# A planner that knows the port shared by two engines: new assumptions and a new table of due times in a two-layer attention and feed-forward kernel

## The chip, the cores and the metric

The kernel runs on one core of a Trainium2 chip. A core has five engines that run side by side and meet through semaphores: TensorE (PE) multiplies matrices, VectorE (DVE) and ScalarE (ACT) work elementwise and empty PSUM, GpSimd (POOL) does masks and small things, SyncE (SP) issues transfers. The metric is device time in microseconds (us), as the median of several runs; lower is better.

## What is computed

Four stages follow each other on a sequence of 2048 tokens of width 640, in bf16: an attention layer A, a feed-forward layer B, and both again with the same weights. Each adds to its input.

```python
x = x + _A_ref(_layernorm(x), wq, wk, wv, wo, beta)
x = x + _B_ref(_layernorm(x), w1, w2)        # relu(x @ w1) @ w2, inner width 1728
x = x + _A_ref(_layernorm(x), wq, wk, wv, wo, beta)
x = x + _B_ref(_layernorm(x), w1, w2)
```

Attention has 32 heads of width 20 and cuts the sequence into 4 segments of 512 tokens. Inside a segment it is causal softmax attention. A running memory `M`, `z` of earlier segments is read beside it:

```python
for s in range(N):
    p = _softmax(qs @ ks.T * scale + mask)
    a_dot = p @ vs
    a_mem = (phi(qs) @ M) / (phi(qs) @ z + 1e-06)    # phi(t) = t + 1 if t > 0 else exp(t)
    outs.append(g * a_mem + (1.0 - g) * a_dot)       # g = sigmoid(beta), by head
    M = M + phi(ks).T @ vs
    z = z + phi(ks).sum()
```

## The kernel before

The unit of work is a segment of a layer, so there are eight of attention and eight of feed-forward. For a segment, the steps and their lines are:

- Layer norm: statistics on DVE (L858, L859, L860), the inverse root on POOL (L865, L867), the normalised tokens `xn_tok` on DVE (L871). They are turned into `xnT` by a crossbar transpose that SP issues (L847), or in the first segments on PE (L835, with an eviction at L842 on DVE or L843 on ACT).
- Projections on PE: keys and queries (L941; evicted at L928 on DVE or L929 on ACT), values (L988; evicted at L976 or L977). A projection fills five tiles; spare rows of these carry the heads of three further tiles, which a DMA through memory moves to partitions of their own (the relay, L1023 and L1036; in the first segment PE does it, L1086).
- Scores on PE in bursts of four or eight small matmuls (L1280), 160 rounds in all. Each round fills four PSUM banks, X and Y, which two exponentials on ACT (L1291, L1294; 128x1024) empty into `PT`. POOL then cuts the causal triangle (L1270). Four heads' worth is multiplied with the values in a burst of sixteen matmuls (apply, L1362), evicted (L1384 or L1390 on DVE), turned by a crossbar transpose (L1461), normalised on DVE (L1396, L1404, L1409) and added to the memory's part (L1414).
- Memory: keys turned by the crossbar (L1117, L1125), `phi` on ACT and DVE (L1133, L1134, L1136), the product on PE (L1143) and its sum and mask on DVE (L1160, L1163). The read is `phi` of the queries (L1196, L1198, L1200), a product (L1230) and DVE steps (L1215, L1218, L1219).
- Output projection: the result `o_sb` turned into `oT` (L1516, crossbar; L1483 on PE in the first segment), PE (L1526), addition to `x_sb` on DVE (L1468).
- Feed-forward: first product (L1580, and L1592 for the rest of 64 columns), relu on DVE (L1561) or ACT (L1562), second product (L1610), addition on DVE (L1468). The second layer's result is stored by SP (L1570).

Three PSUM banks (MISC) serve all other PE work in turn; X and Y together hold one round of scores. Much of PE's work can thus only start once an eviction has freed a bank.

The order on every engine is fixed before the program exists. A planner (`Sched`) takes all steps as streams of `Op`s, each with one or more possible engines and an assumed duration. It keeps a model time per engine, and again and again places the `Op` that can start first; among equals, the one with the earliest due time. Evictions may go to DVE or ACT, whichever ends first in the model. The due times come from `TABLE`, a compressed list with one number for each `Op`, made before. On the chip no model time matters: each engine takes its instructions in the planned order and waits on semaphores where needed. What the planner assumes therefore acts on the kernel through the order and the choice of engine alone.

The assumptions that matter here: a PE step can start `SEM_NS + PE_MARGIN` after the results it reads (60 + 80 ns); a crossbar transpose occupies SP for `XB_NS + XB_TILE` per tile and lands `XB_LAT` after its turn on the DMA; between `LOAD_FROM` and `LOAD_TO` (15 to 125 us of model time) every transfer of SP takes `LOAD_LAT` longer; the relays move 85 bytes per ns. Where PE would have nothing to do, `_filled` puts multiplications of the identity (L769).

The step in which an `Op` gets its model start is in `_best`:

```python
for k, (e, hold, tail, make) in enumerate(op.alts):
    r = ready + SEM_NS + (PE_MARGIN if e == "pe" else 0.0)
    start = rank = max(self.free[e], r)
```

Of the kernel before, what the change touches and what calls it, by code (L numbers as in the profile page):

```python
# [10 lines left out]
ACT = mybir.ActivationFunctionType  # L11
ALU = mybir.AluOpType

T = 2048
# [120 lines left out]
class Op:  # L135
# [4 lines left out]
    def __init__(self, alts, waits, acq=(), users=1, mode="full", dma=None, early=0.0, hold=()):  # L140
        self.alts = alts
        self.waits = [t for t in waits if t is not None]
        self.acq = acq
        self.hold = hold
        self.users = users
        self.mode = mode
        self.dma = dma
        self.due = -1.0
        self.early = early
        self.patience = PATIENCE  # L150

# [7 lines left out]
PE_MARGIN = 80.0  # L159

XB_NS, XB_TILE, XB_LAT = 200.0, 27.0, 1700.0
# [7 lines left out]
LOAD_FROM, LOAD_TO, LOAD_LAT = 15000.0, 125000.0, 4000.0  # L169
# [18 lines left out]
class Sched:  # L188
    def __init__(self, prog, dues=None):
        self.P = prog  # L190
        self.dues = dues
        self.free = {e: 0.0 for e in ENGS}
        self.t = {}
        self.events = {}
        self.fresh = []
        self.active = []
        self.waiting = {}
        self.cur = None
        self.count = 0
        self.ids = set()  # L200
        self.dma_free = 0.0
        self.mode = "full"
        self.log = []
        self.now = -1.0
        self.fill = None
# [71 lines left out]
    def _best(self, op, resv=None):  # L277
# [10 lines left out]
        for k, (e, hold, tail, make) in enumerate(op.alts):  # L288
            r = ready + SEM_NS + (PE_MARGIN if e == "pe" else 0.0)
            start = rank = max(self.free[e], r)  # L290
# [36 lines left out]
    def run(self):  # L327
        while True:
# [45 lines left out]
            if e == "pe":  # L374
                self.mode = op.mode
            if op.dma is not None:
# [29 lines left out]
c-m!JTaX>qb={}?_U(K7zUR*SCC!W^MglzmNyZopA!IP-86XA>31FvUr$~i-  # L406
n4(+`0jE;=%tstk{z?3i4=PTPj{xOVQnno1<%*wFAWA|J4A@vivOpt&n3raD)?VjyPmicuw{Lf!bN1P1pZ!>SpZgJaiPYsTi6xO==}uffD}5P~
*R&%OcuM7CxW-bInhfBsCOy21WKKRRnLL8~7WyC4E70Rkv?gdfu2<piR?r<spBF(jlf!6lqV3nZA8l7l1J5m4(Svxp7T;}XJq0SMT!yDirsaK|
$DKV5qhBmLakriGMfmK+-CoXTboYRsjcrN=&-
?Jb5<F*k8j&q{KM!6iGANg0#4g@<WenHt_{K6SH(>lH@IJwqD?oQQ#`G}DFLgJ5cjJ8rJ@<fCUABUHl{{?0??=!!APaf}*0fbVj`4NO@wz^U_a  # L410
@B-=r2(^+tIR9oV=;K@N{XA$2cg=VE!1Kw&jF=3ZwT>+76@d!mL-Jt%hGGN5R!7XRgS{&uo?3z}fF(O?QCyb+TXX$EvTEYvdM4?Rt#68{bE8|6
6hp@Alx`Zn+8V_WnM(L~h5}+aZUKp~pku{VqKJId=0Xr2ix+-
Y=g4#lvz4d_RcqmoeiV7=2VeCEq{$NpLv>&e~XqNqdKUZ8afpP8Ri9v}TZU1)o$@6Iq8wHNvj+W0P(hb63%)jyW56YNKZYK0A=)F|27A(wW1xh
t?EQPGu5%*nr$mqE{1?2GL^-pDRdX0&QKq@8HR_tBIB$;eHqT4L}ZU&>V;4NAWoT-ffTD=(h#hXTL{r-
GezQkkmHx+=*)kYaRy=BcM0{T7&qVlfR|bk6?x_^n4!Uy5PA3inE{{qkl?GO{nJ$NGYZ5*iM@EOrl4G>uh-5C2wgYQ+T(e6=?e~B-
q9C5au3%R$L;h`T(qK6q+`UUVV96cYyCLxId};<bU<3yr-
u93BJ$k{aD#yd0A&*i!<P>haITVZX@iDlOqcec!~KGagU<nDZfU1>)6t!okYC1H>xq)WA1j$w~j5<VwAOHfvO9m9kn_R^ds7<ze~b+-
_z60M{IEAO3$@Yiz|3`@>TwJNx53AE9ap?4mM_UK@L$dd(3skp)Kzf72h~~^ZBYJ36^<G_@;G{RBdD$_=rmLM)b9QbS3=u!hHG2dRRd|&bS=n+
^>-9g#Ior@##Mq-
k#Qo`?fJ}y(E?Qb)eYS3fJU{^>5ylsPx_yys75vNJ={rZ<2|ZX(LdK3w>DwPfOY;_Gv@^&cX(w(tbz9SkFny`%_xw{N}yi(Uek1*j@|L^w(EmF  # L420
;%Y6Bz-|`?7CLyYrQ__>s+I(1`0VpgZ?Iy;jn(=y#vX6eyTwW%-%Qag`YQ<Wu>(8jXm-+=PQmk*-
Uwq*GcOgmn3WL>uTEE7Qddj(2QJKwM{b3@698}AJW2&JvCbPI|xrS2Jh3rx58MLOCTxsv{vXv6n3X<;|Vpef}M}V&-pXGk%+<-
dRpa5j)1ERTBondZDy7{Rw#iQ{e`XZu>3c!7qrE7)C13Lc+U59vhW8+Nj3L+l^~t`H!AJANw>Ml;^RVRtA%{xLaR6YPA=zW$wzGXmZ?H6^+2tL
_`kjIKbtk)ufbC_%`^@>!Gc}j(^0y$5Bb$N_#t<Z9d*N9TOP;NVyW4h3%1cH_NiU0FD<yK0|{-+YP)xu(Z~EnpS0h@ep#el4EEo^o-
}Arxkryn@<>SCw{G@DuJC-Wh&<jGd0RAlw*L8Z6nw|JHi9mj6?nRFq1UdYleXejb%lRbT8*E@>qaH;S}XZAuY2CR#U-1}C9E2i-
j{vdhDXeMdcE6d@!Yzwx~SN7hii(jUvIu9`>mEVtE`E(@^#qEnl|}1#Y!Xk$GV(>MOYkJ)<LnoGA=&QE@!ET$7@TNuUcsRy1s<IXVth^1J!l(U
e%ar-S1fiUck#-
VXfv#y@o8acMNP20ePves`sp_@9P${pVqg4>Cc0oxbQ&=o);MbI+*1Q5Ka$P^Iy=j|AZwkWAtUfFiniwA^)TwN1vX2pljMA=Lx*<anSx1cwEES
lzK1<4!UR?m!InhaPe_-1K_0wu1@HJCd6Z&yX)n9`VD<ZY&GZAu-
z0gmh0r7^@QGxxu4RrdNtNK2KpvH>$eO&dILNy<823+`2|SfEHK*J;A>cZqyM9ymR~R`ts$<yr>3XB)O+NI`Wu}Cs(cZCYYaRutNFBb$f=H1zp  # L430
Fn0ZaaZ732@yBwVY>&`w$}=t0PZ10ZM1IN(+5oGiquBnEvPFX9_!H+PkJEiBsxh(7OHt`NpbxkDcLpj52!_sL|nlhW<9{EO`2XUJKrAXT~tkh2
T45qS8A0?u75EK^7LH&f)HT9l{z9%1^b%emBa$s?jvRyAND7Ad9=@`?>^5yMb_RMJwQIRlljf2Rf$jHLSY}4HyT-I_RFH?mI?m^LjU9*I&hR7d
ZSy^jHD^r}S-Tr~`!*9Bo7Y3v4-y-R^^eL;iAt>qxn}6|^pE!d!6~JfEjFoX3jK>VJTLTj4ppH{G&`vIrd+gm%4)-
=6?kdrN#?Zz{aRvD1d{tHAuD;Mua533(WrVA8eRvcc?Q8X3hLGm|E;_<e|_mc3kuY$*jI%P_tZGMg^?EUD!=bMX+obPN7C!_IcNzt6c{pl$hh4
-{G$H!Y{#E3k(BXdlP>K5~h^yx^L+cCnj%(9DokjL7kYM!=PueOMW{<vyh!T6{E4idep;9&N=$ZytN?mzOk0%2ilojrrau8RacwsRxuB%a#JM<
lZVO@se|vZSr&*SgBgVE8dI7;xV4d|7!5&GmdtMP+8$KZB(m>WgB#p!iU$%b3R+6h;=@~R6%oDSJdO)Dq>-
t^Ndqc)?*}Khq#mr!~w0Ql4G?zGSmv(-zuV#_3jk$>UeY{P->8Ozot$JgKw6h3!KIUK8RUWXcKAVSzNW?!7)$IrT-UhOF(F8m~DV^*;!yqKcYs
C&1TAUmbFV%6BQbhkIE6&|G}yUik#{>cV%f;|6P41=qVm#blw>vn$7EV&gW_g@s(e(kD>h_izH-2Eh435Vtb$0Jm#(`vc#x_0_vq*am18m-
0X;~l1&IY4fs3XfzhB3aagfQ?$L!<o&?WF<N^6@xf{OvPWiN4CG)V}hvf!2gl{HaU#+3HMXEltn{$wXMT8o6_}B0@Z|Q#WI1L_tgcViE(TZ9{W
s!b2;hf)<*Y!<U#1wY(hlo6f@cv1?j5QIn|7-  # L440
Al3^q6g>ze?_3SayvH2ENFA}#r2{9cDycdFm{Zpiu)W|_m_a1cGJtc(3MXdZ>c52*2Jp0>^X$SA!k<z-
fM3;KL7Za{mQa{0Px@bOST?126x`qt@HGFHYq@?g})+m@tiwrmxot;D01U}<&I&k(J;@+I^g$D7yI_o9z!SPQ*c`0SC4d*<ss+wk;2)WoWX<vZ
)<qYq%VHnIq-JKakU7V}!cY+L2Qv#PW5ntL+ZADwsY=*6W({y{V5lBQLEh~KBR8nmJ&Uk1fTHKCmt509YdS0L9}%5GTpL@lo3TCAzbY-
N&ity9l@EvO4xyRiPd!RI_=c8@lR@2jCcV>|I<y#e%k<iqNQw?tjJ7P~p69;sIuAJdSRT4i<}I@L!8g?R4vvJyL~F?&@oLK*#HW??nPoec83U+
#%c0qYFP5sm5p@;oJFjmiAu60k%A`BqmBI;(;u@+GY^YtN{iNyx&Rlvoe_tS0#Ph|9y6)ugfvFK`@q;287o5oq&kY8Am2ZE9M+h4qhPj>`~(pL
*xn$}RC1q65*nXpg(X-
Me6ZbRyKC%nlDzPXCB+M*FK_tkv=S>h26VX2R?w3i)a(H@SqB$^?A2Ibxdoc{Md{ka56}RfIjX>r;IH827?F#@j#%Ci5qvm^HvQ`fX<fx6h#b5
$BpB!gyLNXS)(T-qCNOkFVJ_Aju}HoMv&~;kZ7f_Z3=nkCyZq$Y4P3p*F2C;*Ak=JVwh|V+3o_>-8x6UGO_6Y2AkI2jwpKn-Tda^h<Syk}w}_U
hoL?at3I`YLiXszv;mc_?y5S!>pTLO7Gdl4mIT`;Cc>rw2L}uh~Kn0LtjHzqu`~1wsmbX78=(66INzZIp#jc_;r}FGavK`eC_OD0`0b+eR|$L_
<0VV@~r+2_hLVNT_3(7f*nt>=dEHHMu(M^gP8X(>B}a#?^EEji*?@%&WF&~By%k}J<qyPk6Jk`dl&wOduZ{z2X9no^i42w1grTx-kL@Y<IPxz3  # L450
l-Y?lia&4M0eYYxHXBW)__mXf+wv~t9&f8SaX}y8GT!L+Ckmx(&kS=-
*007R;Zf$cxE#na)*f5Dp=_t_bUb+JMEYP?z@r*$|}sM?4yR6T~*<iA42~cB10R$^C1$Nk6zT<=(&gJXJcB0=YI;?b{8m(!YW(X-
yvxB9&&HIkI5b6y-#ay;+^-
$kIM(|)xlv8Emf}Pl(XLq^kT8y_^zwaC(dAX!=Ur0ZV+6Xga=rqf85P5)4LJ!p2dnTa~)z_v%j7^FW*8hv+wI!tG-
UY?S8Bt`&!&z)qh*qT>XuU3P4_C@@OY5)tPgAl?6;uu4}*LTtKpUHXfC#;~O>O{)Z~hNx;C-rYh*OE-ETOaZ&M!OVnMc=z5;&QY+PAqk!{z0i8
zjMOO(pC=0cnC7mkj*R6ubj5g*Zx~TqC2`hI2`#t6^XkMXM(`rE6Nm0=~qaIOBGJ09hhYJioT~s}0i)!DDi%K<ZFUeNmu3E}5W&&Dmmw4OY^qE
joj&bMfF!83UTwW7R3;Z_AJZUi4o6%Zkb)%e3*ooX%v0ls9JFG(Fxrmq91!kBPdbu;&W^{ZB*k%@Y3u^JH1~1%a&N~ikw{c%zFpq1vwu-
DbkvYWq1F)j!o#Ch<`G&LH=YTxnrr^i6%gb(5?t}gR0b-_MuvV1f?WA1t?y_1w_6Bxi9NfQ-ym$@syo8K&8#sGKP2LuZ6U67s@tMM`qjGHB{9s
hnS0i{rt1dQqI_P)~nov&Wjou_~>I0o5j5D|4JC8B9yOeLnm^&r%j<aeUu##)>yy|PDu}_|HReJ6*thoc5-
5q6&kfX5YN%T445?b6Sqv<vBR}1s-  # L460
IhR9vTgC2%c>Xm9X|>tEOQbf=yln?^#hqf6nsaJC*pTZ8`mR9o7a;X9YWghpb%qgj5Y}&z$o%G#TCQ8+`E(U`hNh-Dass_<%rsWBit9MWPKW0e
(7O_`csp9QqQ!jpB)HrP9tJVfDyU9k?kVtV5y7|`!mf;?#jx`Q9VPDR5xq=d<Q!J9s1vL{P4ZN-%?v)GhpeO5Hu4kkd~#X0FuJse5PPf-
^umd9AM-EjrSQ`gP_{Kq;yQ&{9nr)HD5RWa6}?t;p5C^Pwb^NQ#90%bZjUnJOaKqBfWK*;L@w$iEN}_WqoBHlr$Z(w;7F`>kn?+a4>Iy+@YcrZ
EcmYx4VdJc;LdAdg*YK$l)9jY@H__({ef1`B%yX~RE9!T=Tfw1(&33<hj_V8k5r?s849XXZ@a-CR@m00h7S<I)p+jMlG8-
fDRsHYQ`SscL`3KG4XqGW**^|EO0N>PrUAG3lh=$`yw1FBmb7Z@mr~;gh!irSDy!LLpx9(fO1^94uSOKo;Cia$A?8d8*Xd6<GR~3)WZIyW_*zA
s@zi63Dq9lfYB4D#lw6B6JYx0lnxTJ-
e%w%Ag%XIlhJ?|mOG)^QKP8PibGLeN>fE4Ia=hFru1Vm(9;zVqP|ay`R4e2>epHjI$bvuakeepGaEJUh_%027+TuM%lQZ9p9JLmDSXAnTtlsaZ
Rcu?~A0~rX%`*MFjsK}0Eig!poMenLRmwh>oIiKV&qjS)CE$U2(1jM`QlIyhZB)XJn%oSxw8JWzVFf*Af0dARbQoV-
# [22 lines left out]
def dve_ns(n, mode):  # L491
    return 66.0 + n / (0.96 * mode)
# [1212 lines left out]
```

## Time and profile before

| | us |
|---|---|
| median of 3 runs | 570.12 (569.62 to 570.35) |
| the profiled execution | 570.93 |
| its span, first to last instruction | 569.2 |

| engine | line | work | count, mean ns |
|---|---|---|---|
| PE | L1610 | second product of the feed-forward | 896, 299 |
| PE | L1580 | first product | 520, 380 |
| ACT | L1294, L1291 | exponentials of the scores | 320, 1025 to 1032 |
| POOL | L1270 | causal masks | 256, 687 |
| DVE | L1468 | additions to x | 128, 479 |
| DVE | L871 | normalised tokens | 64, 529 |
| DVE | L1561 | relu | 50, 666 |
| DVE | L928 | evicted keys and queries | 48, 685 |
| DVE | L1409 | normalised attention | 24, 877 |

A span is what the program's own instructions cover. The time of a run has some 1.7 us more around it. Matmuls overlap, so that their mean durations add up to more than the time they take; the distance between the starts of neighbours tells the pace. The clock granted to TensorE was 1.00 throughout. The crossbar transposes into `xnT`, `oT` and `otok` landed 2.6 to 5.8 us after the start of their issue (median 2.7 to 3.1, by kind).

### The profile page before, as it was taken

The numbers are of one execution on the slowest core, as the hardware profiler recorded it, in microseconds if no ns is written. First come the engines' busy times: TensorE is split into PE (matmuls) and PEld (weight loads), VectorE is DVE, ScalarE is ACT, GpSimd is POOL, SyncE is SP. The second block draws the span as 40 slices with busy tenths as digits, with TensorE's granted clock in tenths as the row PEclk, the third lists the DMA queues.
The fourth block names the chain that finished last, engine by engine and source line by source line (L and its number), as shares of the span: only waits on it lengthen the run. The fifth ranks groups of instructions, "written<-read, shape, count | busy, mean of one in ns | idle before, by whom it ended". The sixth has DMA issues, their size and how long they took to land.

```text
span 569.2 us, 12508 instructions
## 1 busy us (share of the span) xinstructions
PE 558.4 (98%) x5113; PEld 296.0 (52%) x5113; DVE 425.8 (75%) x1020; ACT 424.5 (75%) x519; POOL 215.4 (38%) x343
## 2 busy tenths in 40 slices
PE   8999999999999999999999999999999999999998
PEld 4454445445554445645446554564444654656655
DVE  6689999999999869876689964898767872725202
ACT  4899899998889978778888887977898677332140
POOL 4374447544444434443334423524233422302000
PEclk9999999999999999999999999999999999999999
DMA  6436859766343446454146831386313820432201
GB/s 219 119 89 144 158 123 156 224 150 109 66 91 70 62 71 88 83 97 80 29 77 112 128 43 20 56 122 105 59 21 62 136 69 1 77 81 43 69 0 47
DMA packets 126609, 50.62 MB, mean 89 GB/s; under 512 B 112120, under 2 KB 124600, under 8 KB 126552
## 3 DMA queue, kind: packets, MB, share of 16 engines
q1 hardware_dynamic: 124568, 42.19, 40.7%
q0 software_dynamic: 1552, 7.29, 4.6%
q8 instruction: 40, 0.66, 0.5%
q10 hardware_dynamic: 432, 0.34, 0.2%
q14 instruction: 17, 0.14, 0.1%
HBM read 15.16 MB, written 7.37 MB: 40 GB/s over the span
## 4 chain that ended last, share of the span: by engine, by line
PE 79%; DVE 12%; ACT 4%; DMA 3%; POOL 1%; issue 1%
PE ps L1610 18%; PE ps L1580 17%; PE ps L941 12%; PE ps L1280 7%; PE ps L1526 7%; PE ps L988 7%; PE ps L1362 6%; ACT PT L1294 2%; DMA oT<-o_sb 2%; DVE xn_tok L871 1%; DVE stats L858 1%; DVE x_sb L1468 1%; DVE stats L859 1%; PE ps L1143 1%; PE ps L1230 1%; DVE ktok L1136 1%
## 5 line engine op out<-in xcount | busy, mean ns | idle before, releaser
L1294 ACT ACTIVATE PT<-ps 128x1024 bf16<-128x1024 f32 x256 | 248.3, 1025 | 46.8 <-PE ps L1280 45.9
L1270 POOL TENSOR_SCALAR_AFFINE_SELECT PT<-PT 128x512 bf16<-128x512 bf16 x256 | 171.5, 687 | 262.7 <-ACT PT L1294 218.4
L1610 PE MATMUL ps<-wb,hT 128*128 128x320 bf16 x896 | 136.2, 299 | 1.0 <-DVE x_sb L1468 1.0
L1580 PE MATMUL ps<-xnT,wb 128*128 128x512 bf16 x520 | 126.8, 380 | 0.2 <-DVE hT L1561 0.2
L1468 DVE TENSOR_TENSOR x_sb<-x_sb,ps 128x320 bf16<-128x320 bf16 x128 | 60.7, 479 | 69.9 <-PE ps L1610 47.3
L1610 PEld LDWEIGHTS ps<-wb,hT 128*128 128x128 bf16 x896 | 83.2, 98 | 39.3 <-issue 7.6
L1580 PEld LDWEIGHTS ps<-xnT,wb 128*128 128x128 bf16 x520 | 48.0, 98 | 57.8 <-issue 7.0
L1291 ACT ACTIVATE PT<-ps 128x1024 bf16<-128x1024 f32 x64 | 62.5, 1032 | 14.4 <-PE ps L1280 14.1
L1562 ACT ACTIVATE hT<-ps 128x512 bf16<-128x512 f32 (+1 forms) x62 | 36.1, 583 | 43.6 <-PE ps L1580 42.8
L941 PE MATMUL ps<-xnT,wq_p 128*128 128x512 bf16 x200 | 57.3, 380 | 0.3 <-DVE o_sb L1219 0.3
L988 PE MATMUL ps<-wv_r,xnT 128*128 128x320 bf16 x320 | 57.2, 300 | 0.0
L941 PE MATMUL ps<-xnT,wk_p 128*128 128x512 bf16 x200 | 56.0, 380 | 0.0
L1526 PE MATMUL ps<-wo_r,oT 128*128 128x320 bf16 x280 | 51.8, 299 | 1.2 <-DMA oT<-o_sb 1.1
L1362 PE MATMUL ps<-PT,va 128*32 128x128 bf16 (+3 forms) x896 | 40.8, 302 | 0.0
L988 PEld LDWEIGHTS ps<-wv_r,xnT 128*128 128x128 bf16 x320 | 29.5, 98 | 18.8 <-issue 2.8
L928 DVE CAST kq<-ps 128x512 bf16<-128x512 f32 x45 | 30.8, 685 | 11.1 <-PE ps L941 10.7
L1561 DVE TENSOR_SCALAR hT<-ps 128x512 bf16<-128x512 f32 (+1 forms) x50 | 33.2, 666 | 7.1 <-PE ps L1580 6.9
L871 DVE TENSOR_SCALAR xn_tok<-x_sb,mv,rstd 128x640 bf16<-128x640 bf16 x64 | 33.3, 529 | 4.1 <-POOL rstd L867 2.7
L1280 PE MATMUL ps<-kq 20*128 20x512 bf16 (+3 forms) x560 | 35.3, 301 | 0.2
L1526 PEld LDWEIGHTS ps<-wo_r,oT 128*128 128x128 bf16 x280 | 26.4, 98 | 16.1 <-issue 2.1
L858 DVE BATCH_NORM_STATS2 stats<-x_sb 128x6 f32<-128x320 bf16 x64 | 29.5, 465 | 1.8 <-DMA x_sb<-in_A_x_dram 1.5
L1362 PEld LDWEIGHTS ps<-PT,va 128*32 128x32 bf16 x896 | 18.9, 96 | 22.7 <-issue 10.2
(113 smaller groups left out, 626.6 us busy)
## 6 DMA issues: line engine op xcount, KB each, us to landing
kq_scr<-kq SPq DMA_DIRECT2D x28, 120.0 KB
kqL<-kq_scr SPq DMA_DIRECT2D x28, 120.0 KB
out_dram<-x_sb SPq DMA_DIRECT2D x16, 160.0 KB, 1.8
wb<-in_B_w_dram POOLq DMA_DIRECT2D x5, 432.0 KB, 4.3
x_sb<-in_A_x_dram POOLq DMA_DIRECT2D x3, 640.0 KB, 5.2
wb<-in_B_w_dram POOLq DMA_DIRECT2D x2, 640.0 KB, 5.4
kq_away<-hT SPq DMA_DIRECT2D x5, 256.0 KB, 3.2
kq<-kq_away SPq DMA_DIRECT2D x5, 256.0 KB, 3.4
```

Source lines behind the costliest of these rows:

```text
L871: tn, bx = yield dve(D, 4, lambda e, a, t=t: e.tensor_scalar(a, x_sb[:, t, :], mv[:, t, 0:1], rstd[:, t:t + 1], ALU.subtract, ALU.mult), [ ...
L941: fn = lambda e, bank, k=k, w_p=w_p, c=c: e.matmul(bank, w_p[:, k, c * 128:(c + 1) * 128], xnT[:, k_, :, k, :], start=(k == 0), stop=(k == ...
L988: fn = lambda e, bank, k=k, i=i, hf=hf: e.matmul(bank[:, 0:320], xnT[:, k_, i, k, :], wv_r[:, k, hf * 320:(hf + 1) * 320], start=(k == 0), ...
L1270: tm = yield pool(590.0, lambda e: e.affine_select(out=reg, in_=reg, pattern=[[0, 4], [1, 128]], compare_op=ALU.is_ge, fill=0.0, base=0, c ...
L1280: fns.append((lambda e, x=x, j=j, hh=hh, N=N, o=o: e.matmul(ps[:, hh, o:o + N], kq(b, gg[x], 0)[32 * hh:32 * hh + DH, 128 * j:128 * j + 12 ...
L1291: fn = lambda e: e.activation(PT[:, :, 2 * k:2 * k + 2, 1024:1280], bs.ap.rearrange("p h (x t) -> p x h t", x=2), ACT.Exp, scale=SCALE)
L1294: fn = lambda e: e.activation(PT[:, items[0], 2 * k:2 * k + 2, c0:c0 + 512], bs.ap, ACT.Exp, scale=SCALE)
L1362: return [(lambda e, hh=hh, j=j: e.matmul(bank[32 * hh:32 * hh + 32, 128 * j:L], v_flat[b][:, (j * H + 8 * hh + g) * E1:(j * H + 8 * hh + ...
L1468: ta = yield dve(320, 1, lambda e: e.tensor_tensor(xa, xa, bk.ap[:, 0:320], ALU.add), [tk], early=HOT)
L1526: fn = lambda e, bank, k=k, hf=hf, o=ot.ap: e.matmul(bank[:, 0:320], o[:, k, :], wo_r[:, k, hf * 320:(hf + 1) * 320], start=(k == 0), stop ...
L1580: fn = lambda e, bank, k=k, dc=dc: e.matmul(bank, w1_r[:, k, dc * 128:(dc + 1) * 128], xnT[:, k_, :, k, :], start=(k == 0), stop=(k == FC ...
L1610: fn = lambda e, bank, dc=dc, q=q, h=h, hf=hf: e.matmul(bank[:, 0:320], h, w2_r[:, q, hf * 320:(hf + 1) * 320], start=(dc == 0), stop=(dc ...
```

## The change

Five assumptions of the planner change, and the table of due times is replaced by another:

- `PE_MARGIN` 80 to 200 ns; `XB_LAT` 1700 to 2300 ns; `LOAD_LAT` 4000 to 2500 ns; the rate of the relays 85 to 80 bytes per ns.
- A port that DVE and POOL share is in the plan. A DVE `Op` is marked `port` where its assumed mode is 2 or 4 (and so are the copies of `permute`). A marked DVE `Op` starts in the model no earlier than the end of POOL's last compute `Op`, and a POOL compute `Op` no earlier than the end of the last marked one on DVE.

No instruction of the computation is added or taken away. Line numbers after the table shift by 12.

```diff
-PE_MARGIN = 80.0
-
-XB_NS, XB_TILE, XB_LAT = 200.0, 27.0, 1700.0
+PE_MARGIN = 200.0
+
+XB_NS, XB_TILE, XB_LAT = 200.0, 27.0, 2300.0
...
-LOAD_FROM, LOAD_TO, LOAD_LAT = 15000.0, 125000.0, 4000.0
+LOAD_FROM, LOAD_TO, LOAD_LAT = 15000.0, 125000.0, 2500.0
...
+        self.port = {"dve": 0.0, "pool": 0.0}
...
             r = ready + SEM_NS + (PE_MARGIN if e == "pe" else 0.0)
+            if e == "dve" and op.port:
+                r = max(r, self.port["pool"])
+            if e == "pool" and op.dma is None and hold:
+                r = max(r, self.port["dve"])
...
                 self.mode = op.mode
+            if e == "dve" and op.port or e == "pool" and op.dma is None and hold:
+                self.port[e] = end
...
 TABLE = """
...
 def dve(n, mode, fn, waits=(), acq=(), extra=0.0, users=1, early=0.0):
-    return Op([("dve", dve_ns(n, mode) + extra, 95.0, one(fn))], waits, acq, users, early=early)
+    return Op([("dve", dve_ns(n, mode) + extra, 95.0, one(fn))], waits, acq, users, early=early, port=mode > 1)
...
-                                           lambda e, o=o, i=i: e.activation(o, i, ACT.Copy)))], w)
+                                           lambda e, o=o, i=i: e.activation(o, i, ACT.Copy)))], w, port=True)
...
-                        tk = yield dma("sp", scw_sem[z][r], 122880, f, ev + sc.old, rate=85.0)
+                        tk = yield dma("sp", scw_sem[z][r], 122880, f, ev + sc.old, rate=80.0)
```

## The prediction

> **What bounds the kernel.** I read the page first, for the share of each engine, then the stretches of the span, then the starts of the TensorE's instructions.
>
> ```profile
> PE 558.4 (98%) x5113; PEld 296.0 (52%) x5113; DVE 425.8 (75%) x1020; ACT 424.5 (75%) x519; POOL 215.4 (38%) x343
> ...
> PE   8999999999999999999999999999999999999998
> ...
> DVE  6689999999999869876689964898767872725202
> ...
> PEclk9999999999999999999999999999999999999999
> ```
>
> PE is busy almost everywhere, with the full clock granted (1.00 in every stretch). But a busy PE can hide waits, since matmuls overlap: a 128x320 one lasts 299 ns and the next starts 136 ns after it. So I took the usual distance between starts for each pair of forms (512 columns 216 ns, 320 columns 136 ns, 128 columns 56 ns, 84 columns 40 ns; 95 ns more ahead of a burst of scores or applies) and added them along the program: **550.8 us**. The first matmul starts at 1.24 us, the last one 3.1 us before the end. The span of 569.2 leaves 14.0 us in which PE started later than it could. Of these, 12.0 us are 42 waits of over 25 ns; the other 2.0 are some 10 ns at many of the 691 matmuls that carry a wait. By stage:
>
> | us of the span | 0-16 | 16-50 | 50-120 | 120-190 | 190-360 | 360-460 | 460-569 |
> |---|---|---|---|---|---|---|---|
> | PE waits, us | 3.41 | 1.13 | 2.10 | 2.15 | 0 | 3.16 | 0 |
>
> The program's span plus 1.7 us around it is the profiled execution's 570.93 us, 0.8 over the median of 570.12. Nothing but these 14.0 us can be won, since the change computes the same thing.
>
> Which engine makes PE wait? The stretches (busy us of PE, PEld, DVE, ACT, POOL) say where each has no room:
>
> ```profile
> 50.00:120.00 70.00, 68.91 (x715) 33.46 (x707) 66.27 (x158) 65.48 (x78) 37.54 (x60) 1.00 0.78 166
> 120.00:190.00 70.00, 68.82 (x708) 36.69 (x701) 68.00 (x162) 61.48 (x71) 30.92 (x46) 1.00 0.49 91
> 190.00:360.00 170.00, 170.00 (x1629) 87.94 (x1630) 132.50 (x300) 139.74 (x166) 68.96 (x103) 1.00 0.43 71
> ```
>
> From 120 to 190 us DVE is busy for 68.0 of 70 us; from 190 to 360 for 78%, and there PE waits for nobody. The timeline shows how one such wait is made:
>
> ```profile
> 155.14 1.30 POOL L1270 TENSOR_SCALAR_AFFINE_SELECT PT<-PT 128x512 bf16<-128x512 bf16 x2 [2.16 <-ACT PT L1294]
> 155.19 0.75 DVE L1414 TENSOR_TENSOR o_sb<-o_sb,otok 128x320 bf16<-128x320 bf16 x1
> ...
> 155.87 0.87 DVE L1468 TENSOR_TENSOR x_sb<-x_sb,ps 128x320 bf16<-128x320 bf16 x2
> ...
> 156.40 0.58 PE L1610 MATMUL ps<-wb,hT 128*128 128x320 bf16 x3 [0.54 <-DVE x_sb L1468]
> ```
>
> A mask on POOL starts; DVE's addition L1414 starts under it and takes 0.75 us; the PSUM bank behind it is freed late; PE stands still. That is what the change wants its plan to know.
>
> **The change part by part.** It adds no instruction to the kernel but two fillers. It changes the planner's assumptions and its table of due times, so all queues are reordered. What the order of the built program shows, before and after:
>
> *TensorE's own work.* The same matmuls; fillers on the identity 21 to 23 (2 x 56 ns = +0.1 us, and both stand in the start-up, where PE waits anyway); changes of PE mode 400 to 399; matmuls with a wait 691 to 690. With the same distances the sum is 550.9 us. **0.**
>
> *Evictions change engine.* DVE: relu L1561 50 to 52 (4 full ones more, 2 halves fewer), L928 48 to 44, L842 8 to 4, L976 31 to 33, L917 4 to 5. By the rows (666, 685, 478, 483, 684 ns; a half taken as 400) about -1.1 us on DVE; ACT, by its rows, about +2.1 us. The page has each at 425 of 569 us, so the sum hides; only local places count, and they are below. **0.**
>
> *The shared port as exclusion.* The plan now starts a marked DVE instruction only after POOL's last instruction, and the reverse. Of instructions that meet a POOL instruction the duration says whether the chip does this (min/median/max ns):
>
> ```profile
> L1414 DVE TENSOR_TENSOR o_sb<-o_sb,otok x48: 303/316/791, 106.0 to 503.3; 128x320 bf16<-128x320 bf16 x48
> ```
> ```profile
> L1409 DVE TENSOR_TENSOR otok<-otok,rden x24: 801/825/1244, 104.5 to 502.2; 128x640 bf16<-128x640 bf16 x24
> ```
> ```profile
> L740 DVE COPY wq_p<-wb x7: 268/352/361, 12.8 to 14.1; 128x400 bf16<-128x400 bf16 x4, 128x240 bf16<-128x240 bf16 x3
> ```
>
> L1414 goes from 314 ns with POOL idle to 791 under a mask. Over all marked kinds (L871, L1134, L1136, L1198, L1200, L1414; 220 instructions) 53 are stretched, by 16.2 us together; the masks pay 13.5 us above their 634 ns. The old plan knew nothing of either. Here a rule of the Trainium skill speaks **against** the change as written: "SBUF — State Buffer", section on SBUF's two separate sides, gives the shared pair as an exclusive lock that is taken by a DVE instruction in a two-port mode, *or by one with two SBUF inputs* against a POOL instruction that reads SBUF. The change marks by planned mode alone (over 1). So L1409, L1163 and L1404 (mode 1, two SBUF inputs, 48 instructions) stay unmarked. The trace agrees with the rule: 14 of them are stretched, by 4.8 us. The copies L740 are marked, and none of the 12 is stretched although POOL runs beside most. By the rule 21.0 us of stretch ought to be in the plan, by the change it is 16.2, or 77%: lateness is better known, not removed. No duration falls by itself.
>
> *The wider margin* (80 to 200 ns between a result and the PE step that reads it). I took each PE instruction that waits for a DVE or ACT result, the PE work (at the distances above) between the matmul that this result came from and the reader, and took off what that engine does in between. The trace of before shows that about 535 ns must be left: at 480 PE waited 66 ns, at 546 not at all. Under 700 ns were 42 places before, and **18** are after. That is the gain side. The loss side: a planner with less ready work puts a PE step early and lets it wait. Outside the start-up one place had under 350 ns before (0.17 us of wait) and three have after: 977 ns of PE work between two rounds of scores in the stage 120-190, where before PE waited 305 ns at 1967 and not at 2311 (two exponentials L1294 of 1025 ns lie between); and 816 and 881 ns ahead of memory reads L1230, which need about 1020 and 1130 (a DVE addition of 486 or an ACT relu of 597, and the 535).
>
> *Longer crossbar, shorter loads.* A crossbar transpose of 40 tiles was planned to land 3.58 us after the start of its issue (1280+600+1700; 4.18 after). Outside the loading stretch 13 of 97 landings were later than planned, 10 would be now; inside it all 13 landed earlier than either plan. So this moves positions and removes few waits. Relays at rate 80 for 85: 0.09 us each of 56. Queued behind a late crossbar on SP are the next transposes and relays, as before. **0, between -0.3 and +0.3.**
>
> *The new order against each engine's work.* The same counting over long runs. Between a matmul of L1143 and a reader of the relu L1561 in the stage 120-190 the new order has PE work of 24.3 us (58 of L1610, 25 of L1580, 20 of L1526, 20 of L1230, 17 of L1143, four apply bursts, ten rounds of scores) and 69 DVE instructions. At the mean durations of their rows less the 84 ns by which neighbours overlap on DVE, these are 26.2 us (nine L1468 3.6, six L871 2.7, four L1561 2.4, ten statistics 3.9, and so on). DVE lacks 1.9 us. The worst such run before had 25.7 against 25.8 us. Elsewhere the smallest remainder rises more often than it falls (by us of PE work, 40-60: -419 to 668 ns; 60-80: -33 to 126; 360-380: 506 to 821; 400-420: 719 to 879) but falls at 80-100 (329 to -371). It is a count, not a clock: at some lacks of before PE waited for nothing.
>
> **The sum**, PE waits by stage, before to after:
> - 0-16: 3.4 to 3.4 (the transposes there have 336 ns of work ahead for 784, but the same statistics end last; ends 2.8 and 4.3).
> - 16-50: 1.1 to 0.9 (ACT's lack falls from 489 to 344 ns).
> - 50-120: 2.1 to 1.5 (the waits at 65-68 go, -0.7; the new lack at 80-100 takes 0.8 where 0.7 stood).
> - 120-190: 2.15 to 3.4. Lower end 1.9 + 0.45 to be left = 2.3; before, the same count gives 0.5 where 2.15 were measured, so I add two thirds of that excess of 1.65. Upper end 4.0.
> - 360-460: 3.2 to 1.3. One (1.26 at 389.4) is a late landing of oT, the others are DVE results that came late; the ends are 0 and 3.2, and I take 40% of the old.
> - the 10 ns waits: 2.0 to 2.0.
>
> Together 14.0 to 12.5: **-1.5 us**, 569.4 against the profiled 570.93 and **568.6** against the median. That is 0.26% faster, just outside the 0.2% (1.1 us) below which a measurement of this kernel tells nothing from no change.
>
> **The rivals.**
> - *DVE becomes the bound in 120-190* (slower). For it: 97% busy there and the lack of 1.9 us, which no order of PE can hide. Against it: evictions can move to ACT, and the end of it needs only this stage. Price: 4.0 there, 4.3 at the start, the late waits of 360-460 kept: 14.0 + 1.9 + 0.9 = 16.8, or 572.9. It makes the kernel slower beyond the bound as long as the other stages win back less than 1.6 us of these 2.8.
> - *Nothing moves*: collisions of masks with DVE instructions fall differently in every order, so the waits turn up elsewhere: 570.0. For it: two of the worst waits began with a stretched L1414 (155) and a late landing (389), which no order foresees; 190-360 shows that free room, not order, is what avoids waits.
> - *The plan is true now*: 50-120 and 360-460 free of waits, 120-190 at its lower end: 3.4 + 0.9 + 0.5 + 2.3 + 0.3 + 2.0 = 9.4, or 565.5. For it: 42 to 18 tight places.
> - *It does not do what it says* (unmarked L1409 and its like, marked copies that never collide) is part of the first two.
>
> **How the numbers follow.** Forecast 0.40 (0.33 beyond the bound, 0.07 within), true plan 0.12, nothing moves 0.13 (0.10 within, 0.03 slower), DVE the bound 0.35. So faster 0.45, within 0.17, slower 0.38. The forecast's own range is 567 to 570; the range over the cases is 565.6 to 573.0.
>
> **What would show it.** PE's work sum of 550.9 and about 12.5 us of waits; over 2.3 us of them between 120 and 190, at L1580 and L1230 behind DVE; under 1.6 after 360; L1414 still up to 790 ns. Wrong if the waits of 360-460 stay at 3 us, or if a PE form's distance changes.

## The result and the profile after

The changed kernel takes **567.66 us** (median of 4 runs, 567.54 to 567.81) against 569.87 (569.18 to 570.35) for the kernel before, run beside it: a ratio of 0.9962 with a 95% interval of 0.9945 to 0.998, or 2.2 us less (1.1 to 3.1 by the interval). The span of its profiled execution is 566.0 us. (The profiled execution of before, with its 569.2, stands 1.1 us above this median; so the two traces differ by 3.1 us, and 0.9 of that is not the change.)

The page of after, engine totals and the strips that stood ahead of the prediction:

```profile
PE 557.1 (98%) x5112; PEld 297.0 (52%) x5115; DVE 419.1 (74%) x1018; ACT 426.5 (75%) x523; POOL 208.9 (37%) x341
...
PE   8999999999998999999999999999999999999997
...
DVE  6688989998999777877779956798697865634202
...
PEclk9999999999999999999999999999999999999999
```

Two things are to be seen. DVE has 6.7 us less busy time and POOL 6.5 us less, although they do the same work but for a few evictions: instructions have become shorter (which ones is shown below). And TensorE is "98% busy" in both, which says nothing of a gain. The stretches of after (columns: stretch, its length, then busy us and count of PE, PEld, DVE, ACT, POOL; granted clock; DMA share; GB/s) show where it lies:

```profile
50.00:120.00 70.00, 68.74 (x715) 34.01 (x707) 64.62 (x156) 66.92 (x80) 37.78 (x61) 1.00 0.75 167
120.00:190.00 70.00, 67.63 (x688) 35.51 (x688) 64.39 (x159) 62.04 (x72) 29.94 (x45) 1.00 0.54 90
...
360.00:460.00 100.00, 100.00 (x993) 55.87 (x990) 81.82 (x206) 80.22 (x94) 36.68 (x59) 1.00 0.49 82
```

From 120 to 190 PE now does 688 matmuls where it did 708. From 360 to 460 it is without a gap and does 993 where it did 950 (97.86 us busy before, the same clock). The waits of PE, counted by the distances between starts as in the prediction, say the same by stage. The count was made again for both traces in one way, with the distances inside bursts taken from each trace; that puts the waits of over 25 ns of before at 11.8 instead of 12.0 us.

| us of the span | 0-16 | 16-50 | 50-120 | 120-190 | 190-360 | 360-460 | sum | 10 ns waits | PE without waits |
|---|---|---|---|---|---|---|---|---|---|
| before | 3.41 | 1.05 | 2.03 | 2.15 | 0 | 3.16 | 11.8 | 1.64 | 551.4 |
| forecast (prediction) | 3.4 | 0.9 | 1.5 | 3.4 | 0 | 1.3 | 10.5 | 2.0 | 550.9 |
| after | 2.97 | 1.26 | 1.67 | 3.50 | 0.07 | 0 | 9.5 | 1.53 | 550.6 |

Part of the first column is no wait. The warm-up matmuls (L810, L822 of after) start 427 ns apart at first and 216 ns later, and the slow ones last 634 ns for 379:

```profile
L810 PE MATMUL ps<-ktok x14: 379/462/634, 1.2 to 5.5; 128*128 128x512 bf16 x14
```
```profile
L822 PE MATMUL ps<-ktok x14: 379/634/635, 1.2 to 6.0; 128*128 128x512 bf16 x14
```

So TensorE ran at half pace up to 4.2 us in before and 5.4 us in after, although the row PEclk has full marks there. This is 1.40 us of the 3.41 and 1.99 us of the 2.97; the waits proper at the start fell from 2.0 to 1.0 us.

**The shared port.** DVE's addition and normalisation of after (minimum, median, maximum ns):

```profile
L1426 DVE TENSOR_TENSOR o_sb<-o_sb,otok x48: 266/317/755, 104.2 to 490.9; 128x320 bf16<-128x320 bf16 x48
```
```profile
L1421 DVE TENSOR_TENSOR otok<-otok,rden x24: 804/822/1286, 102.7 to 489.0; 128x640 bf16<-128x640 bf16 x24
```

The worst case is as long as before, so collisions are not excluded. But they are fewer. Of the marked kinds 37 instructions are stretched by more than 60 ns, by 10.8 us together (53 and 16.2 before); of the unmarked L1421, L1175 and L1416, 10 by 2.7 us (14 and 4.8). The masks pay 9.8 us above their 634 ns (13.6).

**The landings.** The tile oT of the kernel before, what its first reader waited for, and its landing times:

```profile
DMA oT<-o_sb: 3.1, 4
...
DMA to landing us min/median/max: 2.6/2.7/5.6
```

and the same view of after, where no line of PE's or PEld's idle time names this transfer any more:

```profile
DVE otok L1421: 0.2, 1
...
DMA to landing us min/median/max: 2.6/2.6/5.7
```

The landings are no faster; they are wanted later. Between landing and the first matmul L1538 that reads it, the eight oT tiles from 360 to 460 us had 0.13, 1.49, 0.05, 1.44, 1.62, 1.66, 0.05 and 0.80 us before, and have 2.2, 15.5, 9.4, 2.4, 3.6, 3.4, 4.2 and 8.1 us after. The two places with 0.05 were waits of 1.26 and 0.22 us.

**The new waits** are in the stage 120-190, and the timeline of after shows the two largest (start, duration, engine, line, operation; in brackets the idle time before it and who ended it):

```profile
169.21 0.81 DVE L1421 TENSOR_TENSOR otok<-otok,rden 128x640 bf16<-128x640 bf16 x1
...
169.95 0.47 DVE L1480 TENSOR_TENSOR x_sb<-x_sb,ps 128x320 bf16<-128x320 bf16 x1
...
170.48 0.81 PE L1155 MATMUL ps<-va,ktok 128*128 128x84 bf16 x16 [0.71 <-DVE x_sb L1480]
...
172.20 1.94 ACT L1306 ACTIVATE PT<-ps 128x1024 bf16<-128x1024 f32 x2 [0.69 <-PE ps L1292]
172.34 0.73 PE L1374 MATMUL ps<-PT,va 128*32 128x512 bf16 x16 [0.17 <-POOL PT L1282]
...
174.19 0.40 PE L1292 MATMUL ps<-kqL 20*128 20x384 bf16 x8 [1.12 <-ACT PT L1306]
```

At 170.5 the memory product needs a bank that DVE's addition L1480 frees late (875 ns by the count of distances). Then two exponentials of 1.94 us together start at 172.20, and PE has just one apply burst of 0.73 us to do before it needs their banks again: it stands for 1192 ns.

### The profile page after: what moved, and what is told of

The parts are those of the page before. It is cut to its first block, busy times and chain, and to the rows that moved or that the text cites. A ratio compares the mean times of both kernels' runs of the same rounds, so it can differ in the third digit from the quotient of the medians.

```text
span 566.0 us, 12510 instructions
## 1 busy us (share of the span) xinstructions
PE 557.1 (98%) x5112; PEld 297.0 (52%) x5115; DVE 419.1 (74%) x1018; ACT 426.5 (75%) x523; POOL 208.9 (37%) x341
## 4 chain that ended last, share of the span: by engine, by line
PE 88%; DVE 7%; ACT 4%; DMA 1%; issue 0%; DVEq 0%
PE ps L1622 20%; PE ps L1592 20%; PE ps L953 14%; PE ps L1292 8%; PE ps L1000 8%; PE ps L1538 7%; PE ps L1374 7%; ACT PT L1306 3%; PE ps L1155 1%; PE ps L1242 1%; DVE x_sb L1480 1%; PE ps L1604 1%; DVE ktok L1148 1%; DVE stats L870 1%; DVE stats L871 1%; DVE xn_tok L883 1%
## 5 line engine op out<-in xcount | busy, mean ns | idle before, releaser
L1282 POOL TENSOR_SCALAR_AFFINE_SELECT PT<-PT 128x512 bf16<-128x512 bf16 x256 | 167.8, 671 | 255.3 <-ACT PT L1306 211.4
L1480 DVE TENSOR_TENSOR x_sb<-x_sb,ps 128x320 bf16<-128x320 bf16 x128 | 61.2, 482 | 79.2 <-PE ps L1622 55.1
L1574 ACT ACTIVATE hT<-ps 128x512 bf16<-128x512 f32 (+1 forms) x60 | 34.4, 575 | 51.9 <-PE ps L1592 51.2
L1303 ACT ACTIVATE PT<-ps 128x1024 bf16<-128x1024 f32 x64 | 62.5, 1030 | 10.4 <-PE ps L1292 10.3
L953 PE MATMUL ps<-xnT,wq_p 128*128 128x512 bf16 x200 | 55.1, 380 | 0.1
L1538 PE MATMUL ps<-wo_r,oT 128*128 128x320 bf16 x280 | 49.5, 300 | 0.0
L1573 DVE TENSOR_SCALAR hT<-ps 128x512 bf16<-128x512 f32 (+1 forms) x52 | 35.1, 680 | 11.3 <-PE ps L1592 10.5
L940 DVE CAST kq<-ps 128x512 bf16<-128x512 f32 x40 | 27.3, 686 | 11.6 <-PE ps L953 11.3
L1538 PEld LDWEIGHTS ps<-wo_r,oT 128*128 128x128 bf16 x280 | 26.2, 98 | 15.9 <-issue 3.1
L883 DVE TENSOR_SCALAR xn_tok<-x_sb,mv,rstd 128x640 bf16<-128x640 bf16 x64 | 31.1, 501 | 3.4 <-POOL rstd L879 1.7
```

The source lines that it names most:

```text
L883: tn, bx = yield dve(D, 4, lambda e, a, t=t: e.tensor_scalar(a, x_sb[:, t, :], mv[:, t, 0:1], rstd[:, t:t + 1], ALU.subtract, ALU.mult), [ ...
L953: fn = lambda e, bank, k=k, w_p=w_p, c=c: e.matmul(bank, w_p[:, k, c * 128:(c + 1) * 128], xnT[:, k_, :, k, :], start=(k == 0), stop=(k == ...
L1282: tm = yield pool(590.0, lambda e: e.affine_select(out=reg, in_=reg, pattern=[[0, 4], [1, 128]], compare_op=ALU.is_ge, fill=0.0, base=0, c ...
L1303: fn = lambda e: e.activation(PT[:, :, 2 * k:2 * k + 2, 1024:1280], bs.ap.rearrange("p h (x t) -> p x h t", x=2), ACT.Exp, scale=SCALE)
L1480: ta = yield dve(320, 1, lambda e: e.tensor_tensor(xa, xa, bk.ap[:, 0:320], ALU.add), [tk], early=HOT)
L1538: fn = lambda e, bank, k=k, hf=hf, o=ot.ap: e.matmul(bank[:, 0:320], o[:, k, :], wo_r[:, k, hf * 320:(hf + 1) * 320], start=(k == 0), stop ...
```

## The experiments

All times are medians beside the kernel before on the same chip (569.65 to 569.87 in these comparisons). "Plan's end" is the model time at which the planner's last step ends. It is not a time of the chip, but the difference between it and the span says how true the plan is. "Stretched" is the sum over the marked and over the unmarked kinds as above.

| kernel | time, us | ratio [95%] | span | plan's end | span less plan | PE waits | PE without waits | stretched |
|---|---|---|---|---|---|---|---|---|
| before | 569.87 | | 569.2 | 558.8 | 10.4 | 11.8 | 551.4 | 16.2 / 4.8 |
| after | 567.66 | 0.9962 [0.9945, 0.998] | 566.0 | 564.8 | 1.2 | 9.5 | 550.6 | 10.8 / 2.7 |
| e1_new_table | 576.67 | 1.0116 [1.0101, 1.0131] | 574.9 | 569.7 | 5.1 | 13.7 | 554.9 | 18.1 / 3.5 |
| e2_old_table | 582.49 | 1.0211 [1.0192, 1.0231] | 581.0 | 583.1 | -2.1 | 14.8 | 560.2 | 10.9 / 5.7 |
| e7_before_small_masks | 565.03 | 0.9909 [0.9894, 0.9924] | 563.4 | - | - | 6.3 | 551.4 | 0 / 0 |
| e8_after_small_masks | 566.23 | 0.9931 [0.9916, 0.9946] | 564.6 | - | - | 7.5 | 551.3 | 0.7 / 0 |
| e3_no_port | 573.59 | 1.0079 [1.006, 1.0098] | 571.8 | 568.5 | 3.3 | 13.4 | 552.5 | 18.3 / 3.3 |
| e4_margin_80 | 578.87 | 1.0167 [1.0143, 1.0191] | 578.5 | 573.9 | 4.6 | 17.2 | 554.9 | 11.5 / 3.1 |
| e9_margin_190 | 573.1 | 1.0075 [1.0052, 1.0099] | 573.0 | 570.3 | 2.7 | 12.0 | 555.1 | 10.4 / 3.9 |
| e10_before_margin_90 | 571.99 | 1.0042 [1.0022, 1.0063] | 570.7 | 560.3 | 10.5 | 13.2 | 551.5 | 17.9 / 4.9 |
| f1_margin_190_retabled | 570.23 | 1.0011 [1.0002, 1.0021] | 568.4 | 567.1 | 1.3 | 10.8 | 551.7 | 12.7 / 3.0 |
| f2_no_port_retabled | 572.24 | 1.0044 [1.0029, 1.0059] | 570.5 | 567.6 | 2.9 | 12.0 | 552.6 | 17.2 / 3.5 |
| f3_margin_80_retabled | 580.25 | 1.0202 [1.0165, 1.0239] | 577.4 | 566.9 | 10.5 | 16.3 | 555.0 | 10.3 / 2.7 |
| f4_port_rule_retabled | 570.47 | 1.0014 [0.9998, 1.003] | 568.7 | 568.9 | -0.1 | 9.3 | 553.6 | 10.2 / 1.8 |

In the profiled executions of e4 and e9 the granted clock was 0.50 for 3.4 us, which adds about 1.7 us to their spans and to "span less plan" (see the last section); the median of e9 is free of it.

### One half of the change without the other

The kernel before, with the new table:

```diff
 TABLE = """
-(the table of before)
+(the table of after)
```

> The planner of before with all its old assumptions, given the new table of due times alone. Theory A (the assumptions put lateness of DVE into the order, the table only ranks what could start at the same time): the late waits after 360 us come back, PE waits 13 to 16 us, time 569.5 to 572. Theory B (the new table carries the gain, the assumptions do nothing): 567.2 to 568.2, no wait after 360 us. Theory C (table and assumptions only work as a pair, since the due times were made from a plan under these assumptions): over 572.

The kernel after, with the old table:

```diff
 TABLE = """
-(the table of after)
+(the table of before)
```

> All new assumptions with the old table of due times. Theory A (assumptions carry the gain): 567 to 568.5, under 1 us of waits after 360 us. Theory B (the table carries it): 569.5 to 571, about 3 us of waits after 360 us. Theory C (only as a pair): over 572.

Each half alone makes the kernel slower, by 6.9 and 12.7 us. In e2 the plan has 167 fillers for 23, and 144 x 56 ns are 8.1 of the 9.6 us by which PE's work without waits exceeds that of after. So table and assumptions are a pair; no part of the 2.2 us can be given to one half.

Two properties do follow one half each. The stretch of the marked kinds follows the assumptions: 18.1 us with the old ones, 10.9 with the new. The slack of the oT landings follows the table: between 360 and 460 us e1 has 0.9 to 15 us of it, and e2 has 0.05, 0.22 and 0.42 at three of the eight, with a PE wait of 1.33 us at the first of these.

### The collisions taken away

The mask covers 8 columns of each 128; the causal cut in the other 120 is left out. The orders stay as they are. A mask then takes 229 ns for 634.

```diff
-out=reg, in_=reg, pattern=[[0, 4], [1, 128]]
+out=reg[:, :, 0:8], in_=reg[:, :, 0:8], pattern=[[0, 4], [1, 8]]
```

In the order of before:

> The kernel before in its own order; each mask on POOL covers 8 of its 128 columns and leaves the causal cut out in the rest, so that POOL holds the shared port for a fraction of the 634 ns. Theory A (stretched DVE instructions make a good part of PE's waits): L1414, L871 and the like keep their undisturbed durations (16 us of stretch gone), waits of 120-190 and 360-460 fall from 5.3 to under 3 us, time 566 to 568. Rival (the order alone makes the waits, the stretch is hidden): waits as before, 569.5 to 570.3.

In the order of after:

> The changed kernel in its own order, with the same small masks (the causal cut left out in 120 of 128 columns). Theory A (the new order already allows for the stretch): it gains less than the kernel before does, 0 to 1 us, to 566.7 to 567.7. Rival (collisions cost both orders alike): it gains as much as the kernel before does from the same edit.

DVE's addition in e7, then its stage 120-190:

```profile
L1414 DVE TENSOR_TENSOR o_sb<-o_sb,otok x48: 306/318/367, 104.4 to 498.1; 128x320 bf16<-128x320 bf16 x48
```
```profile
120.00:190.00 70.00, 70.00 (x726) 38.30 (x724) 63.34 (x162) 63.19 (x74) 13.99 (x46) 1.00 0.54 93
```

and the same stage in e8:

```profile
120.00:190.00 70.00, 68.30 (x708) 36.33 (x708) 61.06 (x159) 62.70 (x74) 13.11 (x46) 1.00 0.51 90
```

No addition is stretched (367 for 791), and the old order has no wait of PE left from 120 to 360. Before gains 4.7 us (569.76 in this comparison to 565.03) and after 1.4 (567.66 to 566.23), each somewhat more than expected. These are upper ends of what the collisions cost, since a mask that is itself shorter also hands PT over sooner and leaves POOL free sooner for the inverse roots of the layer norm. The first counts for little: none of the waits of PE in before stands at an apply (L1362), which reads PT. The second is not separated, but its direct share is small: DVE waits 2.7 us for the roots (L871 behind L867) in before and 1.0 in e7, and 1.7 in after and 0.9 in e8. This is the main reading of the study: long masks cost the old order 4.7 us and the new one 1.4. The difference of 3.3 is more than the whole gain of 2.2, and the remaining 1.1 us is what the new order costs otherwise. With the short masks the old order is the faster one, 565.0 to 566.2. Where the difference between e7 and e8 lies can be seen: in e8 the stage 120-190 keeps 2.33 us of waits, 1.04 of them at the place of 172.8 us, while after 360 it has none. In e7 it is the reverse, 0 and 1.41 us, of which 1.1 (956 and 147 ns) are at L1526, behind oT landings, which shorter masks don't move.

### One assumption undone, the table kept

The port marks left out:

```diff
-    return Op([("dve", dve_ns(n, mode) + extra, 95.0, one(fn))], waits, acq, users, early=early, port=mode > 1)
+    return Op([("dve", dve_ns(n, mode) + extra, 95.0, one(fn))], waits, acq, users, early=early)
...
-                                           lambda e, o=o, i=i: e.activation(o, i, ACT.Copy)))], w, port=True)
+                                           lambda e, o=o, i=i: e.activation(o, i, ACT.Copy)))], w)
```

> The changed kernel without marks for the shared port, the new table kept. C1: 572 to 582, as in the two runs with an exchanged table, and then it says nothing of the port. C2 with the port as what matters: 569 to 571, waits after 360 us back. C2 with the port as a bystander: 567.2 to 568.5.

The margin of before in the kernel after:

```diff
-PE_MARGIN = 200.0
+PE_MARGIN = 80.0
```

> The changed kernel with the old margin of 80 ns, the new table kept. C1: 572 to 582. C2 with the margin as what matters: 569 to 571. C2 with the margin as a bystander: 567.2 to 568.5.

Both are slower than before, by 3.9 and 9.2 us. That looks like the worth of each assumption. Two controls, of 10 ns each, say that it isn't:

```diff
-PE_MARGIN = 200.0
+PE_MARGIN = 190.0
```

> The changed kernel with a margin of 190 ns in place of 200, all else as changed, its table too. After two runs have shown that table and assumptions work as a pair, this asks how close the pair has to be. Theory C1 (the table fits only the exact plan it was made from; any other assumption sends the plan elsewhere): over 570, more fillers. Theory C2 (the table holds nearby, what fell in the two runs was the large step): 567.2 to 568.5.

```diff
-PE_MARGIN = 80.0
+PE_MARGIN = 90.0
```

> The kernel before with a margin of 90 ns in place of 80. C1: over 572. C2: 569 to 571.

A change of 10 ns costs 5.4 us in the new kernel (573.1 against 567.66) and 2.3 us in the old one (571.99 against the 569.65 beside it; just under the 572 that had been expected of a table fitted to one exact plan, and far from no change). A likely reason is that the planner then meets other ties, and due times made for one sequence of choices lead another one astray: e9 has 77 fillers for 23. So what an assumption is worth can't be read from a kernel that keeps the table.

### Each assumption with a table of its own

For each of four sets of assumptions a table was made anew, by random changes of the due times that were kept when the plan ended earlier. None got the plan's end as low as the 564.8 of after; they reached 566.9 to 568.9, so they are compared with each other. The first is the control: after but for a margin of 190.

> Margin 190, all other assumptions as changed, with a table of its own: 50 minutes of random changes of ranks, kept by the end of the plan, from the order of the changed plan. It is the control for the next three, made alike. Its plan ends at 567.1 us of model time, the changed kernel's at 564.8. So far the span on the chip stood beyond the plan's own end by 10.4 us (before), 10.5 (margin 90), 1.2 (changed), 2.7 (margin 190), 3.3 (no port), 4.6 (margin 80 with the port). Theory A (the assumptions decide how true a plan is, the table how short): a gap of 0.5 to 3, time 569.3 to 571.8. Rival (a gap is luck of the order): anything between 569 and 579.

It lands at 570.23, as expected and 2.9 us faster than e9, which has this margin with the table made for 200. It is also 2.6 us slower than after, of which 2.3 are a later end of the plan. The second leaves the port marks out, as e3 does (its margin is 200, so it differs from the control by these 10 ns too):

> No port in the plan, margin 200, a table of its own made in the same way; its plan ends at 567.6. Theory A: DVE is stretched under masks by 16 us or more again (the changed kernel: 10.8, marked kinds), a gap of 3.5 to 7, time 572.8 to 576.3. Rival (port a bystander): about 11 us of stretch or a gap like the control's, time within 1 us of the control plus 0.5.

With nearly the same planned end (567.6 for 567.1) it takes 572.24, **2.0 us more than the control**. Its marked kinds are stretched by 17.2 us for 12.7, and the chip needs 2.9 us more than planned for 1.3 (both the time and this gap stay just under what was expected). This is the cleanest sign that the exclusion in the plan pays. It is one table against one table, though, with a margin 10 ns apart, and the chance in a table has not been measured.

The third has the margin of 80, as e4:

> Margin 80, port in the plan, a table of its own made in the same way; its plan ends at 566.9. Theory A: stretch 10 to 12 us, but many short waits all along, also in 190-360 where the changed kernel has one; a gap of 4 to 7, time 572.6 to 575.6. Rival (margin a bystander): a gap like the control's.

It takes 580.25, beyond all that was expected. That would be a triumph for the margin, had the trace not one wait of 6.5 us in it. The timeline of this kernel:

```profile
103.35 1.06 ACT L1123 ACTIVATE etmp<-ktok 128x1024 bf16<-128x1024 bf16 x1 [6.77 <-DMA ktok<-kq]
...
106.29 0.61 PE L1270 MATMUL ps<-kq 20*128 20x384 bf16 x8 [6.54 <-ACT PT L1284]
```

ACT stands for 6.77 us in front of a key tile that a crossbar transpose brings, the exponentials of the scores are queued behind that instruction, and PE waits for their banks. The tile's own view gives the landing:

```profile
DMA to landing us min/median/max: 2.4/4.3/18.3
```

18.3 us, where the longest for this tile was 9.5 in before and 10.1 in after. In all three it is a transpose issued near 85 us. The stretches around it, 1 us each (the clock is the eighth number):

```profile
102.00:103.00 1.00, 0.00 (x0) 0.00 (x0) 0.00 (x0) 0.00 (x0) 0.00 (x0) 0.97 0.36 102
103.00:104.00 1.00, 0.00 (x0) 0.00 (x0) 0.00 (x0) 0.65 (x1) 0.58 (x1) 0.50 2.01 269
...
109.00:110.00 1.00, 1.00 (x10) 0.24 (x7) 1.00 (x4) 0.60 (x1) 1.00 (x2) 0.61 0.02 6
110.00:111.00 1.00, 1.00 (x9) 0.45 (x6) 1.00 (x3) 0.94 (x2) 0.51 (x1) 1.00 0.00 0
```

The wait also costs the clock. Without these 6.5 us and the 1.7 to 3.3 us that follow it (half of 3.5 us at half clock; the whole excess of PE's work over the control's 551.7) the profiled 577.4 would be 567.6 to 569.2, or 569 to 571 us as a time: like the control. So the worth of the margin isn't shown. What f3 shows is that a landing inside the loading stretch can decide by itself. Whether the margin, the shorter `LOAD_LAT` or the chance of this table put that transfer where it landed late, no run separates.

The fourth marks also what the SBUF rule weighed in the prediction names beside the two-port modes, L1409, L1163 and L1404, and leaves out the copies L740, which the traces show unstretched. Its margin is 200:

```diff
-def dve(n, mode, fn, waits=(), acq=(), extra=0.0, users=1, early=0.0):
-    return Op([("dve", dve_ns(n, mode) + extra, 95.0, one(fn))], waits, acq, users, early=early, port=mode > 1)
+def dve(n, mode, fn, waits=(), acq=(), extra=0.0, users=1, early=0.0, two=False):
+    return Op([("dve", dve_ns(n, mode) + extra, 95.0, one(fn))], waits, acq, users, early=early, port=mode > 1 or two)
...
-                        num, num, rd.ap.to_broadcast([128, 2 * NJ, 4, DH]), ALU.mult), [tr])
+                        num, num, rd.ap.to_broadcast([128, 2 * NJ, 4, DH]), ALU.mult), [tr], two=True)
```

> All assumptions as changed, the marks set by the rule (also L1409, L1163 and L1404 of the kernel before, not the early copies L740), a table of its own made in the same way; its plan ends at 568.9. If the rule makes the plan truer: stretch of the unmarked kinds falls from 2.7 to under 1.5 us, a gap of -1.5 to 1, time 569.1 to 571.6. If 48 instructions do not matter: a gap like the control's and stretch as before.

The unmarked three are now in the plan and their stretch falls to 1.8 us (3.0 in the control, under 1.5 expected). The plan is true: the chip needs 0.1 us less than planned. But a plan with more exclusions ends later (568.9 for 567.1), and the time is the control's: 570.47, with a wait of 1.5 us at the same key tile, late again (13.4 us to landing). Marking by the rule makes the plan truer and gains nothing here.

Nothing that computes the whole result beat the changed kernel's 567.66.

## Why the prediction was right, and where it was wrong

Faster by a little was right, and the time is 0.9 us below the 568.6 predicted. The direction came out partly by luck: the prediction drew its gain from fewer tight places and left the collisions at nothing, and the runs show that fewer collisions are where a gain of this size can come from. By its steps:

- **TensorE's own work, 0:** nearly right; it fell by 0.8 us (551.4 to 550.6, the forecast +0.1). Between kernels with the same order the count itself varies as much (after 550.6, e8 551.3), so nothing is read into it.
- **DVE lacks work time in 120-190, 2.15 to 3.4:** right, with 3.50 measured, though not where most of it was expected, at L1580 and L1230. The 977 ns between two rounds of scores, which need 2270, had to give 1.3 us and gave 1.19. The 816 and 881 ns ahead of the memory reads had to give 0.2 and 0.25 and gave 0.37 and 0.26. The 875 ns at L1155 lie in the run in which DVE was to lack 1.9 us, 26.2 us of its work beside 24.3 of PE's. In after this run took 27.2 us, and DVE was busy for 27.1 of them:

```profile
153.73:180.95 27.22, 25.00 (x274) 13.42 (x271) 27.08 (x72) 23.18 (x26) 13.47 (x20) 1.00 0.44 76
```

  In the stage as a whole DVE has room (64.4 of 70 us). Counting work between a result and its reader, without a simulator, is what worked.
- **The shared port, "lateness is better known, not removed. No duration falls by itself":** this is the step that failed; it left the collisions as they were. The stretch fell from 21.0 to 13.5 us, the masks' from 13.6 to 9.8. A marked step that may not start under POOL loses its place as the step that can start first, and the planner puts another there; so the order itself avoids collisions. (That this is how it comes about is read from the code; that the marks do it is shown by all seven kernels with marks having 10.2 to 12.7 us on the marked kinds, and the five without 16.2 to 18.3, the two with short masks aside.) What it is worth in time is less sure: up to 3.3 us by e7 and e8, which are upper ends, and 2.0 by f1 and f2, one table each.
- **360-460, 3.2 to 1.3:** too high; nothing is left. The prediction took 40% of the old waits as irreducible because a late landing can't be foreseen. The runs show two causes. The DVE part, 1.75 us (3.16 less the 1.41 that e7 leaves), goes when collisions go. The oT part goes because the new table leaves 2.2 us or more between landing and reader, although landings are as slow as ever. So the step on the longer crossbar, "removes few waits", was wrong in effect for oT, though the runs don't tell whether the longer assumed time made the table so.
- **50-120, 2.1 to 1.5, and 16-50, 1.1 to 0.9:** 1.67 and 1.26. In the latter stage the count of ACT's lack promised a small gain and there was a small loss.
- **0-16, 3.4 to 3.4:** 2.97, within its ends; but the waits proper halved, to 1.0 us, and the half pace at the start, which no step counted apart, took 0.6 more.
- **The 10 ns waits, 2.0 to 2.0:** unchanged, 1.64 to 1.53.
- **The wider margin:** 42 tight places to 18 goes with waits that fell from 9.6 to 6.0 us outside 120-190. That the margin did it is not shown (f3), and inside that stage the three bad places (1.8 us together) outweighed the good ones.

Of the rivals, DVE becoming the bound was right in its stage and wrong in the sum, since 360-460 didn't keep its waits. That nothing moves, because collisions fall differently in every order, was wrong: they became fewer. The true plan was nearly right: span less plan fell from 10.4 to 1.2 us. But it was bought with a plan that is 6.0 us longer in its own time. The 9.2 us of lateness that went, less these 6.0, are what the two spans differ by, and 2.2 us of it show in the medians.

## What to carry to other kernels

A static planner that is told of an exclusive resource can do more than know the delays: it orders around them. Look at how many collisions remain, not at the longest one. Ask of each late result how much room its reader has after the landing, and count it in the bounding engine's work: these counts gave the three new waits that they named to within 0.2 us. An assumption of a planner whose due times were fitted to it can only be judged with due times made anew: here 10 ns of one constant cost 2.3 to 5.4 us with the old ones.

## What the runs showed of the hardware

- A DVE instruction that starts under a mask waits for the mask's rest less some 135 ns: L1414 took 434 ns more with 571 ns of mask left, and 277 more with 412. It goes the other way too: one mask took 445 ns more with 585 ns of a DVE instruction left. Masks of 634 ns took up to 1824 in before.
- Additions and products with two SBUF inputs collide although the planner has them in mode 1 (14 of 48 in before), as the Trainium skill, "SBUF — State Buffer", "Who interferes with whom", has it for a POOL instruction that reads SBUF. L1468, L1219 and L1561, which read PSUM, were never stretched, nor were the copies L740, which the change marks.
- The clock answers to a wait of TensorE, and not only to a long one. In f3 PE stopped at 99.7 us; the granted clock fell to 0.50 near 103.0 and came back at 109.8, 3.5 us after PE had begun again at 106.3. The Trainium skill, "TensorE: Matmul & The Clock Gate", Part 1, gives about 3.4 us for both; f3 agrees. But in e9 and e4 the clock was 0.50 for 3.4 us, from 180.6 and from 326.4 us, after PE had stood for only 1.3 and 1.5 us; there the page's idle time does not fit. In e9, the end of the wait and a stretch behind it:

```profile
180.18 0.62 PE L1592 MATMUL ps<-xnT,wb 128*128 128x512 bf16 x2 [1.28 <-issue]
```
```profile
182.00:183.00 1.00, 1.00 (x4) 0.41 (x3) 0.56 (x2) 1.00 (x2) 0.00 (x0) 0.50 0.70 112
```

  Waits of 1.5 us in f4 and 2.0 us in f3 left the clock at 1.00, so the length of a wait alone does not decide. The execution of e9 with the lowered clock took 574.77 us, its others 572.8 to 573.2: some 1.7 us for half the clock over 3.4.
- The crossbar transposes into xnT, oT and otok landed in 2.6 to 5.8 us in before and 2.6 to 7.1 in after, but key tiles in the loading stretch needed up to 9.5 us in before, 10.1 in after, 13.4 in f4 and 18.3 in f3.
